# Attention by query half in a fused attention and Fourier-mixing kernel: score runs of three key chunks, one value run for each half

## The chip, the core and the metric

The kernel runs on one core of a Trainium2 chip. A core has five engines with an instruction queue each: TensorE (PE in the profile; its weight loads are PEld), VectorE (DVE), ScalarE (ACT), GpSimd (POOL) and SyncE (SP), which here only issues DMAs. The metric is the device time of one execution in microseconds (us), taken over three runs, and less is better.

## The reference

```python
def _attn_ref(q, k, v, proj):          # q, k, v: (4 batches, 8 heads, 768, 64), float32
    q_bits = (np.einsum('bhsd,dk->bhsk', q, proj) > 0).astype(np.int64)
    k_bits = (np.einsum('bhsd,dk->bhsk', k, proj) > 0).astype(np.int64)
    q_bucket = np.sum(q_bits * powers, axis=-1)
    k_bucket = np.sum(k_bits * powers, axis=-1)
    mask = q_bucket[:, :, :, None] == k_bucket[:, :, None, :]
    scores = np.where(mask, scale * np.matmul(q, k.transpose(0, 1, 3, 2)), -1000000000.0)
    attn = np.exp(scores - np.max(scores, axis=-1, keepdims=True))
    attn = attn / (np.sum(attn, axis=-1, keepdims=True) + 1e-09)
    return np.matmul(attn, v)

def _moe_ref(x, w_ch1, w_ch2):         # x: (4, 768, 512)
    mixed = np.real(np.fft.fft(np.fft.fft(x, axis=1), axis=2))
    u = x + mixed
    un = (u - mean(u)) / np.sqrt(var(u) + 1e-06)
    return u + np.maximum(un @ w_ch1, 0.0) @ w_ch2
```

A query attends only to the keys whose six sign bits are its own. The heads of a batch laid side by side are the input of the second part, a Fourier mixing followed by a two-layer network.

## The kernel before, in words

**Two streams.** `attention(b)` and `mix(b)` are generators. The main loop at the end of `_main` runs `attention(b)` and, at each of its `yield`s, as many steps of `mix(b-1)` as keep the two in proportion: 24 attention steps (four head pairs, six key chunks of 128 keys) against some 56 steps of the mix. So from batch 1 on the matmuls of the attention stand among those of the network of the batch before. `mix(3)` runs alone at the end. Batch 0 and the start are in a hand-written order (`manual_schedule`); from batch 1 on, the Tile framework's scheduler sets the order of each engine's instructions when the program is built, by priorities (earlier in the program first) and by its own estimate of when each is ready. [...]

**One key chunk of a head pair `n`** (`weigh`, `values`, `attention`). For each query half `g` (384 queries), two matmuls (one per head, 64 rows of the array each, so that the two run side by side) put the scores of both heads into one tile `sc` of two PSUM banks (L893). ACT takes the exponential of it into `pk` (L897, 128x768). DVE then masks: for each head one `scalar_tensor_tensor` over both halves compares the query's bucket `qb` with the key's bucket `kb` and multiplies (L903, 128x768, two for a chunk). Head pairs 0 to 4 (`LITE`) get their mask from an extra bf16 matmul into the scores (L885) and have no L903. DVE adds the chunk into the running sum `acc` (L988, 128x1536). One chunk later the value products follow (`values`, L914): four matmuls, for two halves and two heads, each on half of the array's columns, into `oo`.

**The end of a head pair** (`scale`). ACT copies `oo` into `x` with a bias (L924, L927). Four matmuls on a quarter of the columns each (L932) sum `acc` over the keys. DVE transposes that (L939), adds a small number (L941) and takes the reciprocal `rc` (L942); ACT spreads it by eight small copies (L948, `rr`); DVE transposes back (L949) and multiplies `x` (L953).

**The next head pair's bits** (`prepare`) come in four pieces, one at each of four attention steps: transposes of q and k on DVE (L768) with square sums on ACT (L750), the sign bits by four matmuls (L825) whose result DVE turns into `bt` (L829), and from `bt` the buckets `qb` (L839) and `kb` (L849) by matmuls on 32 rows each.

**Order around it.** `behind()` queues a matmul straight after the last one noted and lifts its priority; the second to fourth score matmuls of a chunk and its value products are put so. [...] two `sc` tiles of two banks, two `oo` banks, and two banks (`ps_1`, given by `pt`) for everything else: the sums, the bits and all products of the mix. In the network, `inner` puts the products p1, p6, p5 and p7 of the first layer (L1390) into these two banks, and p1, p5 and p7 each take a second product on top after ACT has copied out the first (p5's copy is L1422; ACT also evicts the others). `outer7` does the same for the second layer (L1270), evicted in part by ACT (L1289, L1300, L1303) and in part by DVE (L1282, L1316).

Of the kernel before, what the change touches and what calls it, by code (L numbers as in the profile page):

```python
# [11 lines left out]
F32 = mybir.dt.float32  # L12
# [473 lines left out]
def _main(  # L486
# [15 lines left out]
    const = ctx.enter_context(tc.tile_pool(name="const", bufs=1))  # L502
    work = ctx.enter_context(tc.tile_pool(name="work", bufs=2))
    ps_sc = ctx.enter_context(
        tc.tile_pool(name="ps_sc", bufs=2, space=bass.MemoryType.PSUM)
    )
    ps_o = ctx.enter_context(
        tc.tile_pool(name="ps_o", bufs=2, space=bass.MemoryType.PSUM)
    )
    ps_1 = ctx.enter_context(  # L510
        tc.tile_pool(name="ps_1", bufs=2, space=bass.MemoryType.PSUM)
# [8 lines left out]
    def pt(shape, name):  # L520

        turn[0] += 1
        if roomy[0] and turn[0] % 2:
            if turn[0] % 4 == 1:
                return ps_o.tile(shape, F32, tag="o", name=name)
            return ps_sc.tile(shape, F32, tag="sc", name=name)
        return ps_1.tile(shape, F32, tag="ps", name=name)

# [77 lines left out]
    norms = const.tile([P, 2, NPAIR * B], F32, tag="norms", name="norms")  # L606


    NPK = 2
    pks = []  # L610
    for i in range(NPK):
        pk = const.tile([P, 2, 2, HALF + 1], F32, tag=f"pk{i}", name=f"pk{i}")
        nc.gpsimd.memset(pk[:, :, :, HALF : HALF + 1], EPS)
        pks.append(pk)
    sq = const.tile([P, 2, 2, HALF + 1], F32, tag="sq", name="sq")
    ch = const.tile([P, 2, 2, DM // 2], F32, tag="ch", name="ch")
    mean = const.tile([P, P], F32, tag="mean", name="mean")
    nc.gpsimd.memset(mean, 1.0 / (32 * DM))
# [136 lines left out]
    def prepare(n):  # L755
# [66 lines left out]
        ps = pt([P, HALF], f"bits{n}")  # L822
        for j in range(4):
            src = ts["qk"[j // 2]][:, (j % 2) * HALF : (j % 2 + 1) * HALF]
            nc.tensor.matmul(  # L825
                ps[32 * j : 32 * j + 32, :], pj, src, start=True, stop=True
            )
        bt = wt([P, HALF], BF16, "bt", f"bt{n}")
        nc.vector.tensor_scalar(bt, ps, 0.0, None, op0=ALU.is_gt)  # L829
        yield  # L830
# [37 lines left out]
        with tc.issue_after(last[0].ins), tc.high_priority(offset=AHEAD):  # L868
            yield

    def weigh(n, c):

        qt, kt, qb, kb = preps[n]
        ks = slice(c * P, (c + 1) * P)
        heads = [slice(h * D, (h + 1) * D) for h in range(2)]
        pk = pks[npk[0] % NPK]
        npk[0] += 1
        for g in range(2):
            qs = slice(g * HALF, (g + 1) * HALF)
            ps = ps_sc.tile([P, 2, 512], F32, tag="sc", name=f"sc{n}_{g}_{c}")  # L880
            if kb is None:

                at = (c + (NT // 2 if g else 0)) % NT * P
                for h, rows in enumerate(heads):
                    nc.tensor.matmul(  # L885
                        ps[:, h, 0:HALF], qb[rows, 1, at : at + P],
                        qb[rows, 0, g * HALF : (g + 1) * HALF],
                        start=True, stop=False,
                    )

            for h, rows in enumerate(heads):
                with behind() if g + h and n >= NPAIR else nullcontext():
                    last[0] = nc.tensor.matmul(  # L893
                        ps[:, h, 0:HALF], kt[rows, ks], qt[rows, qs],
                        start=kb is not None, stop=True,
                    )
            nc.scalar.activation(  # L897
                pk[:, g, :, 0:HALF], ps[:, :, 0:HALF], AF.Exp, scale=SCALE
            )
        if kb is not None:  # L900
            for h in range(2):
                w = pk[:, :, h, 0:HALF]
                nc.vector.scalar_tensor_tensor(  # L903
                    w, qb[:, h].rearrange("p (g s) -> p g s", g=2), kb[:, h, c : c + 1], w,
                    op0=ALU.is_equal, op1=ALU.mult,
                )
        return pk

    def values(n, c, pk, oos):

        for g in range(2):
            w = HALF + 1 - g
            for h in range(2):
                nc.tensor.matmul(  # L914
                    oos[g][h * D : (h + 1) * D, 0:w], nat["v", n][:, (2 * c + h) * D : (2 * c + h + 1) * D],
                    pk[:, g, h, 0:w], start=(c == 0), stop=(c == NT - 1),
                )

    def scale(n, oos, sums):


        x = xs[n // NPAIR][:, n % NPAIR]
        vs = wt([P, 1], F32, "vs", f"vs{n}")
        nc.scalar.copy(vs, oos[0][:, HALF : HALF + 1])  # L924
        halves = [x[:, g * HALF : (g + 1) * HALF] for g in range(2)]
        for g, xg in enumerate(halves):
            nc.scalar.activation(xg, oos[g][:, 0:HALF], AF.Identity, bias=vs)  # L927

        ps = pt([P, HALF], f"sum{n}")
        for i, part in enumerate(sums):  # L930
            for j in range(4):
                nc.tensor.matmul(  # L932
                    ps[32 * j : 32 * j + 32, :], ones, part[:, j // 2, j % 2],
                    start=(i == 0), stop=(i == len(sums) - 1),
                )


        rt = wt([P, S], F32, "rt", f"rt{n}", 1)
        nc.vector.transpose(rt[:, 0:HALF], ps)  # L939
        rc = wt([P, HALF // 32], F32, "rc", f"rc{n}")  # L940
        nc.vector.tensor_scalar(rc, rt[:, 0:HALF:32], S * EPS, None, op0=ALU.add)  # L941
        nc.vector.reciprocal(rc, rc)  # L942
        yield
        rr = wt([P, 2, HALF // 32], F32, "rr", f"rr{n}")
        for g in range(2):
            for i in range(4):
                j = 2 * g + i // 2
                nc.scalar.copy(rr[32 * i : 32 * i + 32, g], rc[32 * j : 32 * j + 32])  # L948
        nc.vector.transpose(  # L949
            rt.rearrange("p (j i) -> p j i", i=32),  # L950
            rr.rearrange("p g j -> p (g j)")[:, :, None].broadcast_to([P, S // 32, 32]),
        )
        nc.vector.tensor_tensor(x, x, rt, op=ALU.mult)  # L953

    def attention(b):
        xs[b] = wt([P, NPAIR, S], F32, "x", f"x{b}")
        pending, scales = [], []

        def finish():
            n, c, pk, oos, sums = pending.pop(0)  # L960
            with behind() if n >= NPAIR and t is not None else nullcontext():
                values(n, c, pk, oos)
            if c == NT - 1:
                scales.append(scale(n, oos, sums))
                next(scales[-1])

        for t in range(NPAIR):
            n = NPAIR * b + t
            half = fold(b, 0) if t == NPAIR - 1 else iter(())
            if 1 < n + 1 < NPAIR * B:  # L970
                load(n + 1)
            ahead = prepare(n + 1) if n + 1 < NPAIR * B else iter(())
            oos = [ps_o.tile([P, 512], F32, tag="o", name=f"oo{n}_{g}") for g in range(2)]
            acc = wt([P, 2, 2, HALF], F32, "acc", f"acc{n}", 1)
            first = None
            for c in range(NT):
                pk = weigh(n, c)
                new = pk[:, :, :, 0:HALF]
                sums = [acc]
                if c == 0:  # L980
                    first = new
                elif c == NT - 1 and b == 0:

                    sums.append(new)
                else:

                    for g in (0, 1) if b == 0 else (slice(0, 2),):
                        nc.vector.tensor_tensor(  # L988
                            acc[:, g], (first if c == 1 else acc)[:, g], new[:, g],
                            op=ALU.add,  # L990
                        )

                for sc in scales:
                    next(sc, None)
                scales.clear()
                while pending:
                    finish()
                for sc in scales if b else ():
                    next(sc, None)
                pending.append((n, c, pk, oos, sums))  # L1000
                if c > (3 if b == 1 else 2):
                    next(half, None)
                if c > 0:
                    next(ahead, None)
                yield
        t = None
        while pending:
            finish()
        for sc in scales:
            next(sc, None)  # L1010


    HW = HALF // 2
# [55 lines left out]
    def mix(b):  # L1069
# [3 lines left out]


        hd = DM // 2
        F = wt([P, 2, 2, 2, DM], F32, "F", f"F{b}", 1)
        nc.gpsimd.memset(F[:, :, 1, :, 0 : hd + 1 : hd], 0.0)
        for par in range(2):
            for t in range(NT // 2):
# [394 lines left out]
    other = weights1()  # L1474
    next(other)
    nc.sync.dma_start(ch, cn["ch"].ap())
    nc.sync.dma_start(sq, cn["sq"].ap())


    ET = mybir.EngineType  # L1480
    with tc.manual_schedule(engines={ET.PE, ET.DVE, ET.Activation, ET.Pool}):
        for _ in prepare(0):
            pass
        roomy[0] = False
        for i, _ in enumerate(attention(0)):
            if i % 5 < 4:
                next(other, None)
        for _ in other:
# [11 lines left out]
    for b in range(B):  # L1500
        if b > 0:
# [4 lines left out]
            if b == 1:  # L1506
                next(other)
                next(other)
                wait = 2
            steps, done = NPAIR * NT - wait, 2 if b == 1 else 0  # L1510
            for i, _ in enumerate(attention(b), 1):
                if b == 1 and i == 2:
                    for f, avg in means:
                        centre(f, avg)
                while done * steps < (MIX - LEFT) * (i - wait):
# [78 lines left out]
```

## Time and profile before

| what | value |
|---|---|
| three runs | 1100.67, 1101.64, 1103.84 us; median 1101.64 us |
| the profiled execution | 1102.7 us, of which its span is 1100.4 us |
| granted TensorE clock, mean | 0.994 |
| DVE busy in the span | 790.5 us (72%) |
| ACT busy in the span | 499.5 us (45%) |
| span of the attention's score matmuls | first at 11.9 us, last at 890.7 us |
| eight copies `rr`, L948 | 25.2 us in all, 197 ns each |
| DVE steps of 128x256 with three inputs, L1282 `w<-o,rs,w` | x56, 478 ns each |
| load of the table `sq` | 770 KB, once, 10.6 us from issue to landing |

How to read it: a line of the groups names the kernel line, the engine, the operation, what it writes and reads, the tile of the array (rows * columns used) and the shapes, then the count, the busy time and the mean duration in ns, then the idle time before these instructions and what ended it. Matmuls overlap, so their durations add up to more than the time they take; the distance from one start to the next is what counts. In a timeline a line gives start, duration, engine, instruction and count, and in brackets the idle time before it with what ended it.

### The profile page before, as it was taken

How to read it: one execution, taken by the hardware profiler on the slowest of the kernel's cores; microseconds unless marked ns; L12 is line 12 of the kernel's file. 1: busy time of each engine (PE TensorE's matmuls, PEld its weight loads, DVE VectorE, ACT ScalarE, POOL GpSimd, SP SyncE). 2: the span in 40 equal slices, each digit the busy share in tenths (PEclk: the TensorE clock that was granted, in tenths of full speed). 3: DMA queues.
4: the chain of work that ended last, by engine and by line, in shares of the span. 5: the costliest groups of instructions: out<-in, count | busy, mean ns of one | idle time of the engine just before them, and what ended most of it. 6: DMA issues, size and time to landing. Idle time of an engine off the chain costs nothing.

```text
span 1100.4 us, 14144 instructions
## 1 busy us (share of the span) xinstructions
PE 1043.3 (95%) x4933; PEld 632.7 (57%) x4933; DVE 790.5 (72%) x1336; ACT 499.5 (45%) x1055; POOL 58.6 (5%) x132
## 2 busy tenths in 40 slices
PE   7989897999989999999999999999999999999996
PEld 3333353446744675545664576645674569768575
DVE  5899958878599977776767785965856785644353
ACT  6987555553276324454326433355315522340420
POOL 0000000002000020010000011001000002100000
PEclk9999999999999999999999999999999999999998
DMA  9755353451056161322154134213032205122301
GB/s 222 224 95 126 64 140 72 138 164 19 20 149 209 44 204 26 68 63 66 26 157 107 48 82 153 44 43 92 15 129 68 68 24 172 55 81 88 123 20 41
DMA packets 175710, 103.13 MB, mean 94 GB/s; under 512 B 129552, under 2 KB 162960, under 8 KB 175632
## 3 DMA queue, kind: packets, MB, share of 16 engines
q1 hardware_dynamic: 169840, 88.65, 30.1%
q0 software_dynamic: 4224, 13.11, 3.7%
q8 instruction: 41, 0.67, 0.2%
q10 hardware_dynamic: 1568, 0.39, 0.2%
q14 instruction: 37, 0.30, 0.1%
HBM read 81.14 MB, written 20.97 MB: 93 GB/s over the span
## 4 chain that ended last, share of the span: by engine, by line
PE 61%; DVE 11%; ACT 4%; DMA 2%; issue 2%; DVEq 0%; SPq 0%; ACTq 0%
PE o L1270 22%; PE h_p L1390 20%; PE oo L914 6%; PE sc L893 6%; DVE pk L903 3%; PE cs L1086 2%; DMA zraw<-in_moe_w_ch_dram 2%; PE A L1115 2%; PE B L1115 1%; DVE acc L988 1%; ACT rr L948 1%; DVE w L1282 1%; DVE h L1256 1%; PE bits L825 1%; PE un L1141 1%
## 5 line engine op out<-in xcount | busy, mean ns | idle before, releaser
L1270 PE MATMUL o<-w,h 128*128 128x256 f32 x1152 | 259.4, 382 | 1.2 <-ACT tq L1289 0.7
L1270 PEld LDWEIGHTS o<-w,h 128*128 128x128 f32 x1152 | 216.3, 190 | 43.6 <-issue 4.6
L897 ACT ACTIVATE pk<-sc 128x768 f32<-128x768 f32 x192 | 147.6, 809 | 78.4 <-PE sc L893 60.9
L1390 PE MATMUL h_p<-x,w 128*128 128x384 f32 x448 | 163.5, 495 | 3.2 <-ACT h L1412 1.5
L893 PE MATMUL sc<-qt,kt 64*128 64x384 f32 x768 | 155.7, 508 | 6.0 <-ACT pk L897 5.7
L914 PE MATMUL oo<-pk,vn 128*64 128x385 f32 (+1 forms) x768 | 155.3, 499 | 6.0 <-DVE pk L903 3.0
L903 DVE SCALAR_TENSOR_TENSOR pk<-qb,kb,pk 128x768 f32<-128x768 bf16 x132 | 129.0, 1012 | 30.2 <-ACT pk L897 30.1
L1390 PEld LDWEIGHTS h_p<-x,w 128*128 128x128 f32 x448 | 82.3, 190 | 71.0 <-ACT pk L897 5.4
L988 DVE TENSOR_TENSOR acc<-acc,pk 128x1536 f32<-128x1536 f32 (+1 forms) x72 | 105.7, 1482 | 7.2 <-ACT pk L897 6.7
L1390 PE MATMUL h_p<-w 128*128 128x384 f32 x288 | 105.5, 489 | 2.3 <-ACT w L1427 2.3
L914 PEld LDWEIGHTS oo<-pk,vn 128*64 128x64 f32 x768 | 49.1, 136 | 100.0 <-issue 69.3
L893 PEld LDWEIGHTS sc<-qt,kt 64*128 64x128 f32 x768 | 66.9, 188 | 51.3 <-issue 24.0
L1390 PEld LDWEIGHTS h_p<-w 128*128 128x128 f32 x288 | 53.7, 190 | 41.7 <-ACT w L1427 3.5
L1300 ACT COPY tq<-o 128x256 f32<-128x256 f32 x24 | 8.9, 372 | 105.1 <-PE o L1270 105.1
L1282 DVE SCALAR_TENSOR_TENSOR w<-o,rs,w 128x256 f32<-128x256 f32 x56 | 26.7, 478 | 41.6 <-PE o L1270 41.6
L1270 PE MATMUL o<-w 128*128 128x256 f32 x176 | 42.3, 383 | 1.3 <-DVE w L1282 1.3
L1416 DVE TENSOR_TENSOR h<-h 128x384 f32<-128x384 f32 x32 | 17.8, 556 | 33.1 <-ACT h L1415 33.1
L1289 ACT COPY tq<-o 128x256 f32<-128x256 f32 x24 | 8.9, 371 | 69.3 <-PE o L1270 69.2
L1270 PEld LDWEIGHTS o<-w 128*128 128x128 f32 x176 | 32.8, 190 | 8.8 <-DVE w L1282 2.9
L1423 DVE TENSOR_TENSOR h<-h 128x384 f32<-128x384 f32 x32 | 17.7, 553 | 27.0 <-ACT h L1422 27.0
L1024 POOL DMA_DIRECT2D out_dram<-w x30 | 16.4, 548 | 388.7 <-issue 293.2
L1086 PE MATMUL cs<-ch,z 128*128 128x128 f32 (+3 forms) x192 | 33.2, 324 | 3.0 <-DVE bt L829 1.9
(170 smaller groups left out, 1312.4 us busy)
## 6 DMA issues: line engine op xcount, KB each, us to landing
w<-ad SPq DMA_DIRECT2D x168, 128.0 KB, 2.0
w<-bd SPq DMA_DIRECT2D x42, 512.0 KB, 4.5
zraw<-in_moe_w_ch_dram POOLq DMA_DIRECT2D x16, 512.0 KB, 4.0
bd<-w SPq DMA_DIRECT2D x14, 512.0 KB, 3.9
vn<-in_v_dram SPq DMA_DIRECT2D x32, 192.0 KB, 3.4
qn<-in_q_dram SPq DMA_DIRECT2D x120, 48.0 KB, 2.4
kn<-in_k_dram SPq DMA_DIRECT2D x60, 96.0 KB, 3.4
zraw<-in_moe_w_ch_dram SPq DMA_DIRECT2D x8, 512.0 KB, 5.7
```

Source lines behind the costliest of these rows:

```text
L893: last[0] = nc.tensor.matmul(ps[:, h, 0:HALF], kt[rows, ks], qt[rows, qs], start=kb is not None, stop=True,)
L897: nc.scalar.activation(pk[:, g, :, 0:HALF], ps[:, :, 0:HALF], AF.Exp, scale=SCALE)
L903: nc.vector.scalar_tensor_tensor(w, qb[:, h].rearrange("p (g s) -> p g s", g=2), kb[:, h, c : c + 1], w, op0=ALU.is_equal, op1=ALU.mult,)
L914: nc.tensor.matmul(oos[g][h * D : (h + 1) * D, 0:w], nat["v", n][:, (2 * c + h) * D : (2 * c + h + 1) * D], pk[:, g, h, 0:w], start=(c == ...
L988: nc.vector.tensor_tensor(acc[:, g], (first if c == 1 else acc)[:, g], new[:, g], op=ALU.add,)
L1086: nc.tensor.matmul(ps[:, pc + 2 * lo : pc + 2 * hi - 1 : 2], z[:, cp, pc, par, t * P : (t + 1) * P], ch[:, cp, pc, lo:hi], start=(cp == 0) ...
L1115: nc.tensor.matmul(ps[:, cols], F[:, par, k, t, j * P : (j + 1) * P], sq[:, t, k, cols], start=(t == 0), stop=(t == 1),)
L1270: nc.tensor.matmul(ps, a[:, r], right7[i][:, r], start=start and r == 0, stop=r == HF // 2 - 1, skip_group_check=not start,)
L1282: nc.vector.scalar_tensor_tensor(t[:, cols], src, r, t[:, cols], op0=ALU.mult, op1=ALU.add)
L1390: nc.tensor.matmul(ps, left[:, k], right[i][:, k], start=start and k == 0, stop=k == 1, skip_group_check=not start,)
L1416: nc.vector.tensor_tensor(c21, c12, c21, op=ALU.add)
L1423: nc.vector.tensor_tensor(c22, c21, c22, op=ALU.add)
```

## The change

Batch 0 keeps its order in a function of its own, `first_attention`. Batches 1 to 3 go by query half: a head pair is four slots, two for each half. A slot is three key chunks of one half; the value products of a half (all six chunks) stand in one run ahead of the next half's first scores. Masks and sums work on half the width (128x384 and 128x768), twice as many of them. Six half-width `pk` buffers take the place of two full-width ones. `sc` gets a third tile of two banks and `oo` loses its own banks: in batches 1 to 3 it is taken from the two `ps_1` banks through `pt`. The sums and the bits are queued straight behind the last matmul noted. Both last pieces of `prepare`, the bits and the buckets, come in the last slot. The table `sq` loses its buffer of its own; it is loaded by each `mix` on POOL's queue into the end of the tile `F`.

```diff
-        tc.tile_pool(name="ps_sc", bufs=2, space=bass.MemoryType.PSUM)
-    )
-    ps_o = ctx.enter_context(
-        tc.tile_pool(name="ps_o", bufs=2, space=bass.MemoryType.PSUM)
+        tc.tile_pool(name="ps_sc", bufs=3, space=bass.MemoryType.PSUM)
...
-    NPK = 2
+    NPK = NT
...
-        pk = const.tile([P, 2, 2, HALF + 1], F32, tag=f"pk{i}", name=f"pk{i}")
+        pk = const.tile([P, 2, HALF + 1], F32, tag=f"pk{i}", name=f"pk{i}")
...
-    sq = const.tile([P, 2, 2, HALF + 1], F32, tag="sq", name="sq")
...
+            with glued(n <= NPAIR):
+                last[0] = nc.tensor.matmul(
+                    ps[32 * j : 32 * j + 32, :], pj, src, start=True, stop=True
+                )
...
+    def glued(first):
+
+        return nullcontext() if first else behind()
+
+    def weigh(n, g, c, first):
...
+        for h, rows in enumerate(heads):
+            with glued(free or first and h == 0 and kb is not None):
+                last[0] = nc.tensor.matmul(
+                    ps[:, h, 0:HALF], kt[rows, ks], qt[rows, qs],
+                    start=kb is not None, stop=True,
+                )
+        nc.scalar.activation(pk[:, :, 0:HALF], ps[:, :, 0:HALF], AF.Exp, scale=SCALE)
         if kb is not None:
             for h in range(2):
-                w = pk[:, :, h, 0:HALF]
+                w = pk[:, h, 0:HALF]
                 nc.vector.scalar_tensor_tensor(
-                    w, qb[:, h].rearrange("p (g s) -> p g s", g=2), kb[:, h, c : c + 1], w,
+                    w, qb[:, h, qs], kb[:, h, c : c + 1], w,
                     op0=ALU.is_equal, op1=ALU.mult,
                 )
...
+    SLOTS = 4
+
+    def attention(b):
...
+        def finish(free=False):
+            n, g, pk, acc = waiting.pop()
+            oo = pt([P, 512], f"oo{n}_{g}")
+            for c in range(NT):
+                values(n, g, c, pk[c], oo, free)
+            unload(n, g, oo)
+            return scale(n, [[acc[:, i] for i in range(2)]], free) if g else iter(())
...
+            for slot in range(SLOTS):
+                g, run = divmod(slot, 2)
+                glue = bool(waiting) and run == 0
+                totals = finish() if glue else None
...
+                for c in range(run * NT // 2, (run + 1) * NT // 2):
+                    pk.append(weigh(n, g, c, not glue and c == run * NT // 2))
+                    if c:
+                        nc.vector.tensor_tensor(
+                            acc[:, g], pk[0][:, :, 0:HALF] if c == 1 else acc[:, g],
+                            pk[c][:, :, 0:HALF], op=ALU.add,
+                        )
+                for _ in totals or ():
+                    pass
+                if run:
+                    waiting.append((n, g, pk, acc))
+                if slot > 1:
+                    next(half, None)
+                for _ in range((0, 1, 1, 2)[slot]):
+                    next(ahead, None)
+                yield
+        for _ in finish(True):
+            pass
...
-        F = wt([P, 2, 2, 2, DM], F32, "F", f"F{b}", 1)
+        ft = wt([P, 8 * DM + 4 * (HALF + 1)], F32, "F", f"F{b}", 1)
+        F = ft[:, 0 : 8 * DM].rearrange("p (a k t d) -> p a k t d", a=2, k=2, t=2)
+        sq = ft[:, 8 * DM :].rearrange("p (t k f) -> p t k f", t=2, k=2)
+        nc.gpsimd.dma_start(sq, cn["sq"].ap())
...
-    nc.sync.dma_start(sq, cn["sq"].ap())
...
-            steps, done = NPAIR * NT - wait, 2 if b == 1 else 0
+            steps, done = NPAIR * SLOTS - wait, 2 if b == 1 else 0
```

## The prediction

> **What bounds the kernel now.** I read the page first (busy time, then the chain that ended last, then the groups), then busy time by stretch of the span, then timelines of two places in batch 2.
>
> ```profile
> PE 1043.3 (95%) x4933; PEld 632.7 (57%) x4933; DVE 790.5 (72%) x1336; ACT 499.5 (45%) x1055; POOL 58.6 (5%) x132
> ...
> PE 61%; DVE 11%; ACT 4%; DMA 2%; issue 2%; DVEq 0%; SPq 0%; ACTq 0%
> ...
> L893 PE MATMUL sc<-qt,kt 64*128 64x384 f32 x768 | 155.7, 508 | 6.0 <-ACT pk L897 5.7
> L914 PE MATMUL oo<-pk,vn 128*64 128x385 f32 (+1 forms) x768 | 155.3, 499 | 6.0 <-DVE pk L903 3.0
> L903 DVE SCALAR_TENSOR_TENSOR pk<-qb,kb,pk 128x768 f32<-128x768 bf16 x132 | 129.0, 1012 | 30.2 <-ACT pk L897 30.1
> L988 DVE TENSOR_TENSOR acc<-acc,pk 128x1536 f32<-128x1536 f32 (+1 forms) x72 | 105.7, 1482 | 7.2 <-ACT pk L897 6.7
> ```
>
> PE is the bound: 95% busy, most of the chain, and hardly idle before its own groups (6.0 us for all scores). By stretch (columns: stretch and length, then busy time and count of PE, PEld, DVE, ACT, POOL, then clock and DMA):
>
> ```profile
> 120.00:240.00 120.00, 105.85 (x479) 56.28 (x480) 93.57 (x165) 67.25 (x136) 5.57 (x10) 0.97 0.42 120
> 240.00:360.00 120.00, 113.18 (x501) 66.70 (x501) 100.27 (x186) 62.11 (x134) 10.25 (x18) 1.00 0.35 99
> 480.00:600.00 120.00, 118.58 (x514) 70.15 (x513) 83.56 (x133) 50.62 (x109) 4.86 (x12) 1.00 0.35 91
> ```
>
> In batch 1 (about 120 to 385 us) DVE is close behind PE; in batches 2 and 3 PE idles some 1%. What PE loses there lies inside its busy time, at each change of the array's tiling:
>
> ```profile
> 526.73 1.56 PE L893 MATMUL sc<-qt,kt 64*128 64x384 f32 x8
> 528.22 1.51 PE L914 MATMUL oo<-pk,vn 128*64 128x385 f32 x8
> 529.66 3.72 PE L1270 MATMUL o<-w,h 128*128 128x256 f32 x16
> 533.31 1.56 PE L893 MATMUL sc<-qt,kt 64*128 64x384 f32 x8
> 544.66 9.66 PE L1270 MATMUL o<-w,h 128*128 128x256 f32 x44
> ```
>
> The 44 in a row take (9.66 - 0.38) / 43 = 0.216 us each, so the 16 take 3.45 of the 3.65 us up to the next start: 0.20 us for the change. A product of 384 columns takes 0.318 us by the same reading; eight in side-by-side pairs are 1.27 us, against 1.49 and 1.44 between starts: changes of 0.22 and 0.17 us.
>
> The second place shows what waits when ACT is late at the end of a head pair:
>
> ```profile
> 584.61 0.85 PE L932 MATMUL sum<-acc,ones 128*32 128x384 f32 x8
> 586.86 0.23 DVE L942 RECIPROCAL rc<-rc 128x12 f32<-128x12 f32 x1
> 587.37 1.65 ACT L948 COPY rr<-rc 32x12 f32<-32x12 f32 x8
> 589.04 0.84 ACT L750 ACTIVATE sq<-qn 128x768 bf16<-128x768 f32 x1
> 589.88 0.46 ACT L1422 COPY h<-h_p 128x384 f32<-128x384 f32 x1
> 590.40 1.56 PE L1390 MATMUL h_p<-x,w 128*128 128x384 f32 x4 [0.87 <-ACT h L1422]
> ```
>
> The copy that PE needs stands in ACT's queue behind `rr`, and `rr` waits for the reciprocal: PE idles 0.87 us.
>
> [...] the trace has 4.0 us for 512 KB from POOL's queue.
>
> **The change part by part.**
>
> *Fewer tiling changes.* The order of PE's instructions in the two built programs has 363 changes before and 235 after, so the change does what it says. Priced with the median of each kind from the start-to-start distances of the trace: scores to values 90 to 23, at 0.20: -13.4 us; full array to scores 78 to 28, at 0.20: -10.0; values to full 53 to 1, at 0.15: -7.8; all others together (scores to full, values to scores, full to values and scores to sums rise by 22, 20, 17 and 15) +8.7. Sum: -22.5 us, for matmuls that are the same in number.
>
> *DVE's half-width steps.* The form 128x384 of the mask is not in the trace: between 0.48 us (the 256-wide form) and 0.61 (a line through 478 and 1012 ns); in pairs of starts 256 and 768 take 0.44 and 0.97 us, so I take 0.56. The 768-wide sum takes 0.91 in pairs. A chunk costs 4 x 0.56 + 2 x 0.91 = 4.06 us against 3.70; over the 66 chunks with masks +24 us for DVE, 74% of the span. On average that is hidden beside PE.
>
> *Bursts.* What counts is when. Before, a chunk puts 3.7 us on DVE while PE has 3.0 us of scores and values and then two products for the two free banks. Now a slot puts 3 x (2 x 0.56 + 0.91), about 6 us, on DVE at once, and PE's own run of three chunks lasts 1.9 us. Worse, in the first two slots after a values run PE's order is: scores, sums, half a product, scores; two bursts and the end of a head pair come together. I followed the three queues through such a place (inner stage, third head pair of batch 2) with durations of the trace. From the start of the first score run: first exponential 0.97 to 1.78, then every 0.75. DVE from 1.9: six masks and two sums, 5.2, to 7.1; transpose and addition 0.75; a mask 0.56; reciprocal to 8.6. ACT has the eight `rr` (1.65), the sixth exponential (0.75) and p5's copy (0.48) behind it: 11.5. PE comes to p5's second product after run 1.9, sums 0.64, half product 0.64, run 1.9, two products 2.55 and five changes: 8.4. It waits 3.1 us, and 0.2 more for p7. The same walk gives 4.6 us for the second head pair (outer stage, banks freed by L1289's kind on ACT and L1282's on DVE) and 5.0 for the first (copies of p7 and `un`): 4.3 us on average.
>
> *Bits and buckets in one slot.* In the order of DVE `bt` now stands behind nearly the whole burst of the last slot, and the first `qb` matmul follows on PE after 4.8 to 12.2 us counted from the score run; before it came 6 to 11.6 us after the bits, with `bt` done early. A chain 1.9 + six masks 3.4 + two sums 1.8 + `bt` 0.56 = 7.6 us, longer where evictions stand between. In the four head pairs of batch 2 PE is early by 2.9, 1.9, 3.5 and 3.1 us: 11.4.
>
> *`oo` in the two shared banks.* ACT's unloading (0.58 us) lies under the score run of 1.9 us: nothing by itself; it is in the walks. Batch 0 keeps its PSUM places in effect: nothing.
>
> *`sq`.* Off the start: SP's queue is shorter by one load, which PE doesn't wait for. In each mix it is issued on POOL between stores, when `F` is free. In batches 1 and 2 scores and values lie between that and its first use. In `mix(3)` `F` falls free at about 925 us and the first product with `sq` starts at 931.9: 6.9 us for 0.5 of issue and 4 to 6 of transfer. I take nothing; if it took the 10.6 us of the start, 4.
>
> **The sum.** -22.5; waits in the first two slots 9 x 4.3 = +38.7 (three head pairs of each batch); in the last slots 3 x 11.4 = 34.2, of which I take two thirds, +22.8, since a wait earlier in a slot puts PE later at the next; less the idle time that such places have already, 8.2 us of 360 to 900 by stretch, of which I take 6. Together +33.0. The profiled execution of 1102.7 us would become 1135.7; it lies 1.1 above the median, so 1134.6 for the median: 1134 us.
>
> **The rivals.**
>
> [...] If DVE and ACT run ahead of my walks (DVE idles 28% of the span, and nearly no wait of PE is on it now), the 22.5 us come, less up to 12 where batch 1 isn't PE's: 1079 to 1091, about 1087. It decides as soon as a head pair's new waits stay under 22.5 / 11 = 2.0 us; my walks have about 7. For it speaks PE's 95%, against it the two banks, which let PE run only two products ahead. Chance 0.19.
>
> *The two cancel:* waits of about 2 us for each head pair, 1099 to 1105. Chance 0.04.
>
> *DVE becomes the bound in batch 1 as well,* where it has 100.3 of 120 us already: 24 / 3 = 8 us more of it, and all of the last-slot waits (11.4 more) and `sq` (4): 1134 + 23 = 1157 and up to 1175. Chance 0.17.
>
> *My forecast,* waits of 3 to 7 us for each head pair: 1112 to 1157, chance 0.60.
>
> **How the numbers follow.** Slower by over 0.3% (about 3 us, what a measurement of this kernel can tell from no change): 0.60 + 0.17 = 0.77; faster 0.19; within 0.04. The range leaves out half of the first rival and a tail of the third: 1087 to 1166; the forecast's own is 1112 to 1157.
>
> **What would show it.** Right: PE's idle time rises from 57 us to over 100, put down to ACT's copies of p5 and p7 (the group of L1390) and to DVE's evictions and `bt` (L1270, L839); the gaps follow within 12 us of score runs. The distance between starts around a change stays 0.15 to 0.22 us. Wrong: PE idle as before with a span under 1090, or waits of values on masks, which I take to be none since 14 us and more of PE's work lie between in most places.

## The result and the profile after

The changed kernel takes 1160.81 us (median of 4 runs, 1160.03 to 1162.55) against 1102.41 us (4 runs) before: 1.0533 times, 95% interval 1.0512 to 1.0553. The forecast was 1134. The direction is right and the whole range, 1087 to 1166, holds, but the time lies above the forecast's own range of 1112 to 1157, and the loss is 58 us where 33 were worked out. The profiled execution took 1161.09 us, with a span of 1159.3.

From the page of the changed kernel (the busy time of each engine, then the granted clock by slice, the chain that ended last and the groups):

```profile
PE 1044.0 (90%) x4933; PEld 650.8 (56%) x4933; DVE 810.3 (70%) x1528; ACT 500.2 (43%) x1055; POOL 60.8 (5%) x140
...
PEclk9999898999989899999999999999999999999999
...
L900 DVE SCALAR_TENSOR_TENSOR pk<-qb,kb,pk 128x384 f32<-128x384 bf16 x264 | 149.6, 612 | 85.4 <-ACT pk L896 85.4
...
L892 PE MATMUL sc<-qt,kt 64*128 64x384 f32 x768 | 147.7, 499 | 3.8 <-ACT pk L896 3.8
L911 PE MATMUL oo<-pk,vn 128*64 128x385 f32 (+1 forms) x768 | 136.8, 499 | 6.2 <-ACT pk L896 4.2
```

PE's busy time is the same to 0.7 us, although scores and values are cheaper (155.7 to 147.7 and 155.3 to 136.8). What comes on top is idle time: 1159.3 - 1044.0 = 115.3 us, where it was 57.1. The eights in the clock's row are slices (a fortieth of the span each) in which PE was granted 0.80 to 0.90 of full speed on average, where the mean over the span is 0.967; they matter below. Who is waited for, between the start of the first mix and that of the last (line waited for: us in all, times, longest):

```profile
PE qb L834 <- DVE bt L824: 15.4, 8, 3.9
PE A L1168 <- DVE x L1182: 8.9, 7, 3.2
PE h_p L1443 <- ACT h L1465: 7.4, 5, 4.5
PE h_p L1443 <- ACT w L1480: 6.9, 2, 3.4
PE h_p L1443 <- ACT h L1475: 5.8, 3, 2.4
```

The largest is the wait of the buckets on `bt`; then come `A`, a product of the mix that waits for `x`, and the copies that empty the mix's banks (L1465 is p1, L1475 p5, L1480 p7). In the kernel before the largest in this part was another:

```profile
PE sc L893 <- ACT pk L897: 5.7, 3, 2.7
```

Waits of 1.5 us or more in this part number 24; before they were 6. They are not all. Busy time by attention batch, from one mix's first product to the next's, first of the kernel before, then of the changed one (stretch, length, busy time of PE, PEld, DVE, ACT, POOL, then clock and DMA):

```profile
129.40:410.20 280.80, 258.86 (x1166) 155.03 (x1164) 225.74 (x413) 137.53 (x293) 22.90 (x43) 0.99 0.38 111
410.20:669.60 259.40, 255.54 (x1186) 154.23 (x1184) 190.59 (x291) 109.33 (x233) 13.65 (x30) 1.00 0.32 84
669.60:925.00 255.40, 252.19 (x1163) 153.61 (x1162) 185.41 (x286) 102.44 (x217) 13.45 (x28) 1.00 0.24 69
```

```profile
129.00:436.10 307.10, 262.40 (x1186) 162.49 (x1184) 238.69 (x481) 139.88 (x297) 22.01 (x42) 0.94 0.36 104
436.10:713.40 277.30, 256.35 (x1187) 160.79 (x1185) 196.40 (x359) 109.04 (x231) 14.57 (x30) 0.97 0.30 80
713.40:983.40 270.00, 250.01 (x1159) 157.80 (x1158) 190.75 (x353) 101.80 (x216) 14.16 (x29) 0.98 0.23 67
```

All three batches lose (26.3, 17.9 and 14.6 us), the start and the tail (175.4 us before, 175.9 after) nothing. Length less PE's busy time gives the idle time: it rises by 22.8, 17.1 and 16.8 us. And the clock, 0.99 to 1.00 before, is 0.94 to 0.98. One place in batch 1 shows how the two belong together. PE, then DVE, in order of time (start, length, what, and in brackets the wait before it):

```profile
388.74 0.52 PE L820 MATMUL bits<-qt,pj 128*32 128x384 f32 x2 [2.32 <-DVE w L1335]
...
394.67 0.50 PE L834 MATMUL qb<-bt,pw 32*128 32x384 bf16 x2 [3.92 <-DVE bt L824]
...
395.42 3.78 PE L1323 MATMUL o<-w 128*128 128x256 f32 x8
```

```profile
388.61 1.66 DVE L900 SCALAR_TENSOR_TENSOR pk<-qb,kb,pk 128x384 f32<-128x384 bf16 x3
390.19 0.94 DVE L1046 TENSOR_TENSOR acc<-acc,pk 128x768 f32<-128x768 f32 x1
...
394.07 0.54 DVE L824 TENSOR_SCALAR bt<-bits 128x384 bf16<-128x384 f32 x1
```

The same place by stretches:

```profile
390.00:395.00 5.00, 1.08 (x12) 0.29 (x11) 5.00 (x13) 0.00 (x0) 0.00 (x0) 0.50 0.00 0
395.00:400.00 5.00, 5.00 (x15) 3.72 (x12) 4.63 (x9) 1.17 (x2) 0.55 (x1) 0.52 0.27 70
400.00:405.00 5.00, 5.00 (x24) 4.00 (x24) 1.38 (x3) 0.37 (x1) 0.00 (x0) 1.00 0.40 65
```

The bits are done at 389.6, but `bt` runs at 394.07, behind masks, sums and the steps of a fold: DVE is busy all the while. That is the wait foreseen. What was not foreseen is the last number but two of each line: by stretches of 1 us the clock is at half from 389.5 to 399.8, and the eight matmuls of 256 columns from 395.42 to 398.99, the next start, take 0.446 us each, where the prediction read 0.216. They count as busy.

So I split each span in three. Busy time times (1 - clock), summed over stretches of 1 us, is what half clock costs; busy time less that is the work at full clock; the rest is idle.

| kernel | span | work at full clock | idle | half clock |
|---|---|---|---|---|
| before | 1100.4 | 1039.9 | 57.1 | 3.4 |
| changed | 1159.3 | 1013.8 | 115.3 | 30.2 |
| difference | +58.9 | -26.1 | +58.2 | +26.8 |

This is an account of where the span went. How much of the 26.8 us would come back as waiting if the clock had stayed is not shown by it.

### The profile page after: what moved, and what is told of

The parts are those of the page before. It is cut to its first block, busy times and chain, and to the rows that moved or that the text cites. A ratio compares the mean times of both kernels' runs of the same rounds, so it can differ in the third digit from the quotient of the medians.

```text
span 1159.3 us, 14340 instructions
## 1 busy us (share of the span) xinstructions
PE 1044.0 (90%) x4933; PEld 650.8 (56%) x4933; DVE 810.3 (70%) x1528; ACT 500.2 (43%) x1055; POOL 60.8 (5%) x140
## 4 chain that ended last, share of the span: by engine, by line
PE 55%; DVE 25%; ACT 9%; DMA 5%; issue 3%; SPq 2%; DVEq 0%; ACTq 0%; POOLq 0%
PE o L1323 21%; PE h_p L1443 19%; DVE pk L900 9%; PE oo L911 8%; DVE acc L1046 5%; ACT pk L896 3%; PE sc L892 2%; DMA zraw<-in_moe_w_ch_dram 2%; PE cs L1139 2%; ACT rr L951 1%; DVE x L1182 1%; PE A L1168 1%; SPq L571 1%; PE B L1168 1%; ACT sq L744 1%
## 5 line engine op out<-in xcount | busy, mean ns | idle before, releaser
L1323 PE MATMUL o<-w,h 128*128 128x256 f32 x1152 | 264.8, 386 | 10.0 <-ACT tq L1356 2.8
L900 DVE SCALAR_TENSOR_TENSOR pk<-qb,kb,pk 128x384 f32<-128x384 bf16 x264 | 149.6, 612 | 85.4 <-ACT pk L896 85.4
L1443 PE MATMUL h_p<-x,w 128*128 128x384 f32 x448 | 169.6, 507 | 19.6 <-ACT h L1465 7.4
L896 ACT ACTIVATE pk<-sc 128x768 f32<-128x768 f32 x192 | 144.5, 809 | 34.2 <-PE sc L892 33.3
L892 PE MATMUL sc<-qt,kt 64*128 64x384 f32 x768 | 147.7, 499 | 3.8 <-ACT pk L896 3.8
L911 PE MATMUL oo<-pk,vn 128*64 128x385 f32 (+1 forms) x768 | 136.8, 499 | 6.2 <-ACT pk L896 4.2
L1046 DVE TENSOR_TENSOR acc<-acc,pk 128x768 f32<-128x768 f32 x96 | 91.0, 947 | 5.4 <-ACT pk L896 4.9
L1335 DVE SCALAR_TENSOR_TENSOR w<-o,rs,w 128x256 f32<-128x256 f32 x56 | 26.8, 479 | 38.3 <-PE o L1323 38.2
L1353 ACT COPY tq<-o 128x256 f32<-128x256 f32 x24 | 8.9, 372 | 93.7 <-PE o L1323 93.7
L1323 PE MATMUL o<-w 128*128 128x256 f32 x176 | 45.3, 403 | 1.0 <-DVE rt L942 0.6
L925 ACT ACTIVATE x<-oo,vs 128x384 f32<-128x384 f32 x32 | 18.1, 579 | 47.1 <-PE oo L911 46.6
L1139 PE MATMUL cs<-ch,z 128*128 128x128 f32 (+3 forms) x192 | 33.4, 329 | 4.5 <-DVE z L1110 4.3
```

What stands on the lines that cost most here:

```text
L892: last[0] = nc.tensor.matmul(ps[:, h, 0:HALF], kt[rows, ks], qt[rows, qs], start=kb is not None, stop=True,)
L896: nc.scalar.activation(pk[:, :, 0:HALF], ps[:, :, 0:HALF], AF.Exp, scale=SCALE)
L900: nc.vector.scalar_tensor_tensor(w, qb[:, h, qs], kb[:, h, c : c + 1], w, op0=ALU.is_equal, op1=ALU.mult,)
L911: last[0] = nc.tensor.matmul(oo[h * D : (h + 1) * D, 0:w], nat["v", n][:, (2 * c + h) * D : (2 * c + h + 1) * D], pk[:, h, 0:w], start=(c ...
L925: nc.scalar.activation(x, oo[:, 0:HALF], AF.Identity, bias=shift[n])
L1046: nc.vector.tensor_tensor(acc[:, g], pk[0][:, :, 0:HALF] if c == 1 else acc[:, g], pk[c][:, :, 0:HALF], op=ALU.add,)
```

## The experiments

Times are medians; "ratio" is against the kernel before on the same chip.

### Bits one slot ahead of the buckets

```diff
-                for _ in range((0, 1, 1, 2)[slot]):
+                for _ in range((0, 1, 2, 1)[slot]):
```

> The changed kernel with the bits matmuls of the next pair issued one slot before its bucket matmuls again (slot 2 and slot 3), nothing else. Theory A (TensorE stalls make the loss, and each stall of some 2 to 4 us is followed by matmuls at half clock): the 15.4 us that the bucket matmuls wait for bt fall below 3, four or five of the half-clock stretches next to them go, and the time falls by 15 to 25 us, to 1136 to 1146. Theory B (VectorE's backlog after a run of three chunks sets the pace, whatever stands behind it): the same idle time comes back at other matmuls, the waits on bt are replaced by waits on the mix's evictions, and the time falls by less than 6 us, to 1155 or more.

1147.34 us, ratio 1.0399 (1.0373 to 1.0425): 13.5 us less than the changed kernel. No bucket matmul waits for `bt` any more; idle time is 104.5 us, half clock still costs 30.2. The result lies between the theories: the wait is a real part of the loss, but under a quarter of it, and the half-clock stretches did not go with it.

### Masks left out

```diff
-        if kb is not None:
+        if kb is not None and free:
             for h in range(2):
                 w = pk[:, h, 0:HALF]
```

> The changed kernel with the mask instructions of batches 1 to 3 left out (192 VectorE instructions; the scores are then not cut to the bucket, so the output is another). Theory A1 (the bursts that count stand in VectorE's queue, behind the masks): idle time of TensorE falls from 115 to below 65 us, the granted clock rises to 0.99, time 1080 to 1100. Theory A2 (the bursts that count stand in ScalarE's queue: three exponentials ahead of the copies that free the mix's banks, masks or not): the waits on bt go, those on ScalarE's copies (about 25 us) stay, the clock stays at 0.98 or below, time 1115 to 1140.

1109.78 us, ratio 1.0067. Idle 81.9 us, half clock 14.3, mean clock 0.982: between the two theories. Masks in VectorE's queue have a hand in the larger part of the stalls, since 33.4 of the 58.2 us of added idle time go with them and 51 us of the time; but 82 us of idle time stay where A1 gave 65, and the buckets still wait 9.9 us for `bt`, which A2 excluded. This edit takes load off VectorE (678.4 us busy in place of 810.3) as well as bursts; the next one tells the two apart.

### Half-width masks and sums in the kernel before

```diff
-            for h in range(2):
-                w = pk[:, :, h, 0:HALF]
-                nc.vector.scalar_tensor_tensor(
-                    w, qb[:, h].rearrange("p (g s) -> p g s", g=2), kb[:, h, c : c + 1], w,
-                    op0=ALU.is_equal, op1=ALU.mult,
-                )
+            for g in range(2):
+                for h in range(2):
+                    w = pk[:, g, h, 0:HALF]
+                    nc.vector.scalar_tensor_tensor(
+                        w, qb[:, h, g * HALF : (g + 1) * HALF], kb[:, h, c : c + 1], w,
+                        op0=ALU.is_equal, op1=ALU.mult,
+                    )
...
-                    for g in (0, 1) if b == 0 else (slice(0, 2),):
+                    for g in (0, 1):
```

> The kernel before with the masks of batches 1 to 3 in four instructions of 384 per chunk in place of two of 768, and the sums in two of 768 in place of one of 1536, at the same places. Prediction's price: VectorE +20 to 30 us busy, TensorE idle up by 0 to 8 us, time 1100 to 1111. Rival D (VectorE's load by itself, not its bursts, makes the changed kernel slower): idle time up by 20 us or more, half-clock stretches as in the changed kernel, time 1125 or more.

1097.38 us, ratio 0.9956 (0.9941 to 0.9972): faster than the kernel before, and the fastest of all. Two lines of its page, to be held against the changed kernel's:

```profile
PE 1044.0 (95%) x4933; PEld 631.7 (58%) x4933; DVE 811.2 (74%) x1528; ACT 500.1 (46%) x1055; POOL 61.4 (6%) x132
...
L904 DVE SCALAR_TENSOR_TENSOR pk<-qb,kb,pk 128x384 f32<-128x384 bf16 x264 | 150.1, 613 | 18.2 <-ACT pk L897 17.9
```

VectorE has the same load as in the changed kernel (811.2 and 810.3 us) with the same 264 masks, and PE is idle for 50.9 us. The load by itself costs nothing. What costs must be where it falls and what PE has to do meanwhile. That the shorter instructions let PE's evictions through sooner would explain the gain, but this was not tried apart.

### Bits and buckets in one step in the kernel before

```diff
         nc.vector.tensor_scalar(bt, ps, 0.0, None, op0=ALU.is_gt)
-        yield
+        if n <= NPAIR:
+            yield
```

> The kernel before with the bits and the bucket matmuls of a pair in one step (11 pairs, 5 to 15), as the changed kernel has them, nothing else. The prediction's step on them by itself: the bucket matmuls wait 1.0 to 2.5 us for bt in each pair, behind the masks and the sum of one chunk, 11 to 27 us of idle time, time 1113 to 1130 with what half clock adds. Rival: the wait is short there (below 0.6 us a pair), because one chunk's masks are a short queue and only the runs of three make it long: 1101 to 1108.

1106.86 us, ratio 1.0045 (1.0027 to 1.0062): the rival's time. The same step costs some 5 us behind one chunk's masks and 13.5 behind three; the wait on `bt` is 2.9 us in all here, 15.4 in the changed kernel.

### Matmuls put into the waits

```diff
             ps = ps_sc.tile([P, 2, 512], F32, tag="sc", name=f"qb{n}_{h}")
+            for _ in range(FILL.get(n, 0) if h == 0 else 0):
+                with behind():
+                    last[0] = nc.tensor.matmul(
+                        ps[:, 0, 0:HALF], ts["k"][:, 0:P], ts["q"][:, 0:HALF],
+                        start=True, stop=True,
+                    )
```

`FILL` is {5: 7, 7: 4, 8: 6, 10: 4, 12: 6} in the first and {5: 4, 7: 2, 8: 3, 10: 2, 12: 3} in the second.

> The changed kernel with 4 to 7 more matmuls (128x384, into the bank that the bucket matmul then overwrites) ahead of the first bucket matmul of five pairs, where it waited for bt, 26 in all, about 8.3 us of TensorE at full clock: bt comes no earlier, TensorE only works while it waits. Theory A (idle time lowers the clock): the half-clock stretches that followed these waits (317, 389, 543 and 672 us of the trace) go or shrink, 10 or more of 76 us of half clock in all, and the time falls by 3 to 8 us although work is added, to 1153 to 1158. Rival C (the lower clock has another source than the waits): mean clock stays 0.967 within 0.003, the added matmuls cost 0 to 8 us, time 1160 to 1169.

The pricing was wrong: they are 27, not 26, and the trace has two records for each (4987 matmul records in place of 4933). The work at full clock rose by 17.9 us, 0.33 for each record and twice what was meant to be added. 1160.31 us, ratio 1.0527: the time is C's and misses theory A's, while the mean clock, 0.973, lies outside C's. Hence the second:

> As e3_fill_waits with 14 added matmuls in place of 27: two passes of 0.32 us each, 28 records and 9.0 us at full clock, below the waits that they stand in. Theory A (idle time lowers the clock): idle time falls by 6 to 10 us, half clock costs 20 to 26 in place of 30 us, so time falls by 1 to 7 us although 9 us of work are added: 1154 to 1160. Rival C (the lower clock has another source): half clock within 2 us of 30, the added work shows as far as it exceeds the waits: 1160 to 1168.

1155.95 us, ratio 1.0486 (1.0460 to 1.0512): some 5 us less with 9.0 us more work, in theory A's range, though its interval just touches that of the changed kernel; idle time -11.4, half clock 27.6, between the two theories. The total is thus a weak witness, since other half-clock stretches came up elsewhere. The places themselves are clearer, and the last section of this document has a more direct test on all the traces. The four stretches named had 3.4, 10.2, 3.4 and 3.4 us of half clock; in both fillings 3.4, 3.4, 0 and 0 are left. One of them, around the buckets of pair 10, first in the changed kernel, then with the waits filled (PE, PEld, DVE, ACT, POOL, clock):

```profile
540.00:544.00 4.00, 2.27 (x17) 1.69 (x17) 4.00 (x7) 1.17 (x2) 0.00 (x0) 0.89 0.02 4
544.00:548.00 4.00, 4.00 (x15) 3.29 (x14) 2.63 (x6) 0.52 (x1) 0.00 (x0) 0.68 0.00 0
```

```profile
538.00:542.00 4.00, 3.24 (x23) 2.66 (x23) 4.00 (x8) 1.69 (x3) 0.00 (x0) 1.00 0.00 0
542.00:546.00 4.00, 4.00 (x21) 3.08 (x21) 4.00 (x8) 0.37 (x1) 0.00 (x0) 1.00 0.13 22
```

VectorE is as busy as before, much of PE's idle time is filled, and the clock stays.

### Exponentials, masks and sums spread over the slot

The run of three scores stays; `soften` issues the exponential and the masks of one chunk, and a third of the slot's mix steps stands between one chunk and the next. `AHEADS`, the chunks (of twelve a head pair) after which the four pieces of `prepare` come, is (3, 5, 6, 8), so that bits and buckets are two chunks apart. In the second kernel the exponentials are issued at the run and `soften` does the masks alone.

```diff
+                for i, c in enumerate(cs):
+                    soften(n, g, c, ps[c], pk[c], exp=True)
+                    if c:
+                        nc.vector.tensor_tensor(
+                            acc[:, g], pk[0][:, :, 0:HALF] if c == 1 else acc[:, g],
+                            pk[c][:, :, 0:HALF], op=ALU.add,
+                        )
...
+                    if 3 * slot + i in AHEADS:
+                        next(ahead, None)
...
+                    yield
```

> The changed kernel with the same runs on TensorE, but the exponential, the masks and the sum of a chunk are no longer issued for all three chunks at the run: chunk by chunk, with a third of the slot's mix work between one and the next; bits in slot 2 right behind the scores, buckets at the end of slot 2. 233 changes of tiling in the built order against 236. Theory A (bursts in the queues of VectorE and ScalarE make the stalls, stalls make half clock): full-clock work of TensorE stays at 1014 us within 4, idle time falls from 115 to 60 to 80 us, half clock costs below 10 us in place of 30, time 1080 to 1100. Rival E (the values of a half are waited for once the masks come later, so that the stalls move to the value run): idle time 95 us or more, the largest waits at oo on the masks, time 1125 or more.

> As e5_spread_all, but the three exponentials stay together at the run; masks and sums alone are spread. Theory A with VectorE as the queue that counts: within 10 us of e5_spread_all, 1085 to 1105. Theory A with ScalarE's queue as a second one: the waits of the first layer (h_p) on ScalarE's copies, some 20 us in the changed kernel, stay, time 1105 to 1130.

1142.90 and 1142.44 us, ratios 1.0360 and 1.0356. Theory A fell in its simple form: against the kernel with bits earlier only 4.4 and 4.9 us are gained, idle time is 105.6 in both (60 to 80 expected), half clock 19.1 and 17.9. The values didn't wait on masks either. But the test is not clean, since the edit also made a new wait. The bits are put into one of the two shared banks, and products of the mix now wait there until VectorE has made `bt` of them (first kernel):

```profile
PE h_p L1459 <- DVE bt L824: 6.2, 4, 3.0
PE o L1339 <- DVE bt L824: 3.6, 3, 1.5
```

With 2.9 us of `A` this makes 12.7 us, and 12.4 in the second kernel; with bits earlier alone such waits were 1.5 us. Without them some 94 us of idle time would be left by subtraction, still more than theory A gave. What breaking up the bursts is worth while PE's runs stay as long is therefore not settled. That the masks now stand among the mix's evictions, where PE, with no scores left to do, waits, would be a reason for the rest; it was argued and not shown.

### Shorter runs

```diff
-    SLOTS = 4
+    RUNS = 3
+    SLOTS = 2 * RUNS
+    CH = NT // RUNS
...
-                g, run = divmod(slot, 2)
+                g, run = divmod(slot, RUNS)
...
-                for c in range(run * NT // 2, (run + 1) * NT // 2):
+                for c in range(run * CH, (run + 1) * CH):
...
-                for _ in range((0, 1, 2, 1)[slot]):
+                for _ in range((0, 1, 1, 1, 1, 0)[slot]):
```

`RUNS` = 3 makes runs of two chunks; 6 makes runs of one, with the four preparing steps in slots 3, 5, 6 and 8 of twelve.

> The changed kernel with scores in runs of two chunks in place of three (six slots a pair), each run with its two chunks' exponentials, masks and sums; the bits one slot ahead of the buckets as in e1_bits_earlier; values, banks and all else as changed. Built order: 282 changes of tiling against 232 of e1_bits_earlier. Theory A (the length of the bursts sets the stalls): full-clock work of TensorE 1014 + 50 x 0.17 = 1022 us, idle time down from 104 to 70 to 85 us, half clock costs 10 to 20 in place of 30, time 1105 to 1130. Rival F (the shared banks, which the values of a half now hold, make the stalls whatever the run's length): idle time within 8 us of 104, half clock as it was, time 1145 to 1160.

> The same with one chunk of one half in a run (twelve slots a pair). Built order: 418 changes of tiling. Theory A: full-clock work 1014 + 186 x 0.17 = 1046 us, idle time 50 to 65 us, half clock below 8 us, time 1098 to 1120. Rival F: idle time 90 us or more, time 1140 or more.

| scores in a run | time | ratio | work at full clock | idle | half clock |
|---|---|---|---|---|---|
| 3 (bits earlier) | 1147.34 | 1.0399 | 1014.1 | 104.5 | 30.2 |
| 2 | 1131.27 | 1.0269 | 1025.0 | 89.0 | 16.8 |
| 1 | 1115.17 | 1.0127 | 1045.3 | 60.2 | 6.7 |

Shorter runs take most of the stalls away. PE's run, VectorE's bursts and the spread of the mix's steps change here together, so which of these counts is not told apart. With runs of one the idle time is within 3.1 us of the kernel before's, and of the 11.8 us that its span is longer 5.4 are work at full clock: the changes of tiling are back, and half-width runs of one have more of them than before. Runs of two kept somewhat more idle time than expected (89.0 where 70 to 85 were), and another cause was still in place:

### Value runs in the score banks

```diff
-            oo = pt([P, 512], f"oo{n}_{g}")
+            oo = ps_sc.tile([P, 2, 512], F32, tag="sc", name=f"oo{n}_{g}")[:, 0]
```

> e1_bits_earlier with the output bank of each value run taken from the score pool (three pairs of banks) in place of the two shared banks of the mix; runs, bursts and the rest as in e1_bits_earlier. Built order: 251 changes of tiling against 232. Rival F (the value run leaves the mix one bank at a time): idle time down from 104 to 75 to 92 us, half clock 12 to 22, time 1115 to 1135. Theory A, and the prediction's step that the shared banks cost nothing: idle time within 6 us of 104, time 1144 to 1156 (1147 and 19 x 0.17 = 3 us of tiling).

1126.76 us, ratio 1.0233 (1.0201 to 1.0266): 20.6 us less than with bits earlier alone. Idle 88.5, half clock 17.0: rival F's numbers. (The profiled executions lie further apart, 27.3 us.) The shared banks, which the prediction put at nothing, cost about as much as the step from runs of two to runs of three: idle time and half clock fall by 29.2 us here and by 28.9 there, and the intervals of the two ratios overlap. That the mix lacks a second bank while a value run holds one is the reason that led to the run; the run shows the cost of the place, not the reason apart.

### All of them together

Bits earlier, masks spread, runs of two, values in the score banks.

> The three cures together on the changed kernel: bits ahead of the buckets and masks and sums spread over the slot as in e5m_spread_masks, scores in runs of two as in e8a_runs_of_two, value runs in score banks as in e9_values_in_score_banks. Built order: 306 changes of tiling. If the causes found add up: full-clock work 1014 + 70 x 0.17 = 1026 us, idle time 60 to 75 us, half clock 5 to 12 us, time 1092 to 1114. Rival: they are one cause (the same waits cured three times): idle time no lower than the 88 of the best of them, time 1120 or more.

1101.77 us, ratio 1.0005 (0.9992 to 1.0017): as the kernel before. Idle time by batch, in the same view as above:

```profile
412.20:673.10 260.90, 254.41 (x1186) 155.53 (x1185) 196.39 (x359) 110.02 (x233) 15.25 (x30) 0.99 0.33 86
673.10:929.00 255.90, 249.22 (x1164) 153.98 (x1163) 191.65 (x354) 102.79 (x217) 14.70 (x29) 1.00 0.24 71
```

6.5 and 6.7 us are idle where the changed kernel had 20.9 and 20.0. The causes about add up: 13.5 (bits), 20.6 (banks), 16.1 (runs of two) and 4.9 (spreading) make 55.1 us, and 59.0 came back. By the ratios, which take out that the runs were on several chips, it is about 52 of 58. But runs of two keep only 1039.9 - 1027.1 = 12.8 of the 26.1 us of tiling, and idle time and half clock are still 8 and 9 us above the kernel before in the profiled execution, which took 4.9 us more than the median. Nothing is won.

## Why the prediction was right in direction and short by 26 us

*Fewer tiling changes, -22.5.* Right: -26.1 us of work at full clock. The price holds in the other direction too: 50 changes more cost 1025.0 - 1014.1 = 10.9 us, 186 more 31.2, so 0.22 and 0.17 us each. With the work at full clock put down to them, the changes thus had their price in whole kernels here, not only between neighbours.

*Half-width steps, +24 us on VectorE, hidden.* Right on the load (+20.7 us in the kernel before with half widths, 567 ns a mask, from 149.6 / 264); on the time nothing was even too cautious, it gained 5 us. The rival that VectorE becomes the bound by load falls with that; in batch 1 of the changed kernel VectorE is busy for 238.69 of 307.10 us.

*Bursts, and bits and buckets in one slot: 38.7 + 22.8 - 6 = 55.5 us of idle time.* The sum is close, 58.2 us, its parts less so. The waits on `bt` were 15.4 us, and undoing that step gave 13.5. The three places followed in batch 2 were there, but shorter: 2.4 us at p5 in the third head pair (3.1), 1.9 in the second (4.6), 3.4 at p7 in the first (5.0); many smaller waits elsewhere made up for it. The wait of `A` for `x`, in none of the walks, is the second largest. That the sum came so close is thus in part luck.

*`oo` in the two shared banks, nothing by itself.* This step failed. It asked whether the unloading is late for the next product, and not what the mix has left while a value run holds one bank of its two. Value runs in other banks took 16.0 us of idle time and 13.2 of half clock away.

*`sq`, nothing.* Right on the time, since the tail is as long as before. The four loads took 6.9 us (median) from issue to landing, where the prediction had 0.5 for the issue and 4 to 6 for the transfer; in proportion, the 4.0 us that 512 KB took from POOL's queue make 6.0 for these 770 KB. In the tail one product, `A`, waited 0.4 us for the table.

*The sum.* Its failed step is a term that is not in it. It takes the matmuls at one price, however PE waited before, and so each microsecond of idle time at one microsecond. The runs show 26.8 us of half clock on top, which is the whole of what was missing: -26.1 + 58.2 + 26.8 = 58.9 against -22.5 + 55.5 = 33.0. The mean clock of before, 0.994, gave little warning, and the forecast took it as a constant. The measured time lies where the rival "DVE becomes the bound in batch 1" had put it, 1157 to 1175, and that rival's reason is refuted above: that the whole range took in this time is luck.

*What would show it.* Idle time over 100 us, waits on p5, p7 and `bt`, no values waiting on masks: as said. "DVE's evictions" were right too: in batches 1 to 3 VectorE ends 44.8 us of PE's waits (9.8 before) and ScalarE 40.6 (18.0).

## What to carry to other kernels

Grouping matmuls of one tiling saved 0.17 to 0.22 us a change here (26.1 us of work at full clock), but it took away the work that covered the evictions of what runs beside it (58.2 us more idle time): count the saved changes against the waits that come into the stretches between. Price a stall at more than its length where it leaves PE idle for most of 3.4 us; half clock cost 26.8 us more here. Before a stage is given another's PSUM banks, ask what that other stage can do with the banks that remain; the value runs in the mix's banks cost 20.6 us here. And look at load and lateness apart: VectorE was idle for 30% of the span, and PE still waited 3.92 us for its `bt`.

## What was not expected of the hardware

In these traces PE's clock falls to half after idle time that is quite short, 2.32 us in the first example below. The changed kernel has 15 half-clock stretches before its tail, all at 0.50 and of 3.4, 6.8 or 10.2 us. Counted as in the table of spans above, a stretch of 3.4 us in which PE works throughout costs 1.7; in the one at 395 us a product took 0.446 us in place of 0.216. Within one trace all changes of the clock lie on one grid of 3.413 us, to within 0.002 us in the traces of the kernel before and the changed one. So each trace can be cut into such windows, and PE's busy share in a window be held against the clock in the next one. Over the 14 traces of this case, the start up to the clock's first record and the end left out:

| PE's busy share in a window at full clock | windows | next window at half clock |
|---|---|---|
| under 0.40 | 96 | 96 |
| 0.40 to 0.60 | 136 | 15 |
| over 0.60 | 4135 | 0 |

On the way back, of 119 windows at half clock with a share over 0.80, 111 were followed by full clock, and of 36 below that none. This speaks against rival C in all the kernels at once: in these windows the clock went with how busy PE was just before. It also tells waits that brought half clock from waits that did not. Three windows of the changed kernel:

```profile
386.11:389.52 3.41, 1.09 (x10) 0.16 (x9) 3.41 (x7) 0.00 (x0) 0.00 (x0) 1.00 0.00 0
491.92:495.33 3.41, 1.58 (x8) 0.88 (x6) 3.41 (x9) 1.63 (x9) 0.00 (x0) 1.00 0.12 38
495.33:498.75 3.42, 1.82 (x8) 1.06 (x8) 3.35 (x5) 3.28 (x7) 0.00 (x0) 1.00 0.00 0
```

In the first, PE waits 2.32 us up to 388.74, all in one window; the share is 1.09 / 3.41 = 0.32, and the clock is at half from 389.52. The wait of 3.43 us up to 496.93 (p7's copy) is longer, but the grid cuts it in two; the shares are 0.46 and 0.53, and the clock stays. The grid stands differently against the start from trace to trace: its first line is 0.40 us into the span in the changed kernel and 1.02 in the kernel before. As an estimate from the table: more than 0.60 x 3.41 = 2.05 us of idle time in one window lowered the clock every time (96 of 96), less than 0.40 x 3.41 = 1.36 us never (0 of 4135).

Over the kernels tried, idle times of 51 to 65 us went with 3 to 12 us of half clock, 82 to 89 with 14 to 17, and 101 to 115 with 18 to 30. The 58 us of idle time that the change added came with 27 more. What decides in windows with a share of 0.40 to 0.60, of which 15 in 136 were followed by half clock, stays open.
